# A three-stage attention and expert kernel: the second expert's first nine weights held back until the last float64 tile is converted

## The chip, the cores and the metric

The kernel runs on one core of a Trainium2 chip. A core has five engines that run side by side and wait for each other by semaphores: TensorE (PE in the profile; PEld is its weight load), VectorE (DVE), ScalarE (ACT), GpSimd (POOL) and SyncE (SP, which here only issues transfers). The metric is the time of one execution on the device, in microseconds; less is better.

## The reference

Linear attention with decay, then a mixture of experts with capacity, then a dense two-layer network. Cut to what matters:

```python
# attention over t: y_t = r_t (state + u k_t v_t);  state = w state + k_t v_t
x = attn_out.transpose(0, 2, 1, 3).reshape(3072, 384)
# greedy routing: each of 8 experts takes 384 tokens, the highest gate values first
for e in range(8):
    mask = assigned == e
    out[mask] = relu(x[mask] @ w1[e]) @ w2[e]        # 384 -> 1024 -> 384
h = relu(out @ w_in)                                  # 384 -> 2048
return ((h * h) @ w_out)                              # 2048 -> 384
```

The weights w1 and w2 are float32 and each belongs to one expert. The weights w_in and w_out are float64, and all tokens share them.

## The kernel before

The kernel first computes the attention in 24 chunks of 128 tokens. It then takes the eight experts one after the other, in an order that the routing finds out on the way. For each it routes (`phase`), gathers that expert's 384 tokens, runs the expert's two layers (`expert`) and at once the dense network on the same tokens (`mlp`), and scatters the 384 rows to the output.

Every operand of a product is split in two parts: a rounded one (`wh`, `ah`, `YH`, `WI[0]`) and the rest (`wl`, `al`, `YL`, `WI[1]`), the difference to the full value. `mm3` multiplies rounded by rounded, rounded by rest and rest by rounded: lines 836, 837 and 838. A block of one 128-wide column of weights against 384 tokens is nine such matmuls.

**Expert weights.** Each expert has 16 tiles of 128x384 numbers, eight of w1 (`n` 0 to 7) and eight of w2 (`n` 8 to 15). In the list `seq` the first expert has the numbers 0 to 15 and the second 16 to 31. `load_next` issues the next tile's transfer from SP into one of five raw buffers (line 921), as soon as routing knows which expert comes (`known`). `split_next` makes the two parts in one of nine pairs of buffers: the rounded part on ACT (line 832) and the rest on POOL (line 833; the first eight on DVE). It puts both 200 places ahead in the priorities of the planner that orders the queues of ACT, DVE and POOL. SP and PE keep the order in which the program is written. In expert 1 (the second) the block `hmm(1, f)` needs the tile 16+f, and `ymm(1, 0)`, which stands right behind `hmm(1, 2)`, needs tile 24, the ninth.

**float64 weights.** The dense network's weights are 32 tiles of float64 (`wi` 0 to 15 and `wo` 0 to 15, taken in turn). They are turned into float32 once, while the first expert and its dense network run, and are then kept. `fetch` loads a tile from SP (line 856). `convert` has three pieces on DVE (lines 886, 887, and 883 in `join`, which completes the number), then the rounded part on ACT (872) and the rest on POOL (868). `fill` hands out the pieces, three per step in the first expert and two per step in its dense network. A step is a call of `tick`, which also calls `load_next` and `split_next`. Counted through the program, the second expert becomes known in step 32, and the last piece of the last float64 tile is handed out in step 35. Step 38 is followed by the block `gmm` 13 of the first dense network, step 40 by `gmm` 14 and step 42 by `gmm` 15, and expert 1 begins after step 47.

In the dense network the block `gmm(p, f)` needs both parts of `wi` f and `omm(p, f)` those of `wo` f, in the order `omm(0)`, `gmm(4)`, `omm(1)`, `gmm(5)`, ... `omm(11)`, `gmm(15)`, `omm(12)` to `omm(15)`. Between `gmm` and `omm` stand three steps on ACT (1006, 1012, 1013) and one on DVE (1016, `al`). `oev` then scatters three times 128 rows from POOL (1031). The routing of the following expert runs beside all this, mostly in small steps on DVE.

Of the kernel before, what the change touches and what calls it, by code (L numbers as in the profile page):

```python
# [42 lines left out]
FB1, FB2 = 8, 16  # L43
KG = 64
BIG = 1e38
NW, NRAW = 9, 5
# [749 lines left out]
def moe(ctx, tc, a, R, xd, out):  # L796
    nc = tc.nc
    V, G, A_, PE = nc.vector, nc.gpsimd, nc.scalar, nc.tensor
# [14 lines left out]
    now, queue = [-1], []  # L813

    def later(k, fn):
        if now[0] < 0:
            fn()
        else:
            queue.append((now[0] + k, fn))
# [11 lines left out]
    def split(t, hi, lo, eng=None):  # L831
        A_.activation(hi, t, AF.Copy)  # L832
        (eng or G).tensor_tensor(lo, t, hi.bitcast(FT), op=OP.subtract)  # L833
# [7 lines left out]
    WI = [cs.tile([128, FB2, 3, 128], FR, name=f"wi{j}") for j in range(2)]  # L841
    WO = [cs.tile([128, FB2, DM], FR, name=f"wo{j}") for j in range(2)]
    order = [x for f in range(FB2) for x in (("wi", f), ("wo", f))]
    fetched, pieces, rest, done, alive, hold, credit = [], [], {}, set(), [], [False], [0.0]

    def part(w, f, j):
        return WI[j][:, f].rearrange("p k m -> p (k m)") if w == "wi" else WO[j][:, f]
# [12 lines left out]
    def convert(w, f, t):  # L860

        hi, lo = part(w, f, 0), part(w, f, 1)
        wide = t.dtype == I32
        v = t[:, :, 1].bitcast(FT) if wide else t

        def end():
            def finish():
                G.tensor_tensor(lo, v, hi.bitcast(FT), op=OP.subtract)  # L868
                done.add((w, f))
                alive.pop()  # L870

            todo = rest[w, f] = [lambda: A_.activation(hi, v, AF.Copy), finish]  # L872
            go = lambda: todo and todo.pop(0)()
            later(1, go)
            later(2, go)

        if not wide:
            return [end]
        low, high = t[:, :, 0], t[:, :, 1]
        c = ps.tile([128, 512], I32, name="conv", bufs=1)[:, :384]  # L880

        def join():
            V.scalar_tensor_tensor(high, high, -1073741824, c, op0=OP.bitwise_and, op1=OP.bitwise_or)
            end()

        return [lambda: V.tensor_scalar(c, high, 5, 2, op0=OP.logical_shift_left, op1=OP.logical_shift_right),
                lambda: V.scalar_tensor_tensor(c, low, 29, c, op0=OP.logical_shift_right, op1=OP.bitwise_or),
                join]

    def fill(n=1):  # L890
        credit[0] += n
        while credit[0] >= 1:
            credit[0] -= 1
            if not pieces:
                fetch()
                if not fetched:
                    return
                pieces.extend(convert(*fetched.pop(0)))
                fetch()
            pieces.pop(0)()  # L900
# [11 lines left out]
    raws, wt, used, loaded_at = {}, {}, set(), {}  # L912

    def load_next():
        i = len(loaded_at)
        if i >= len(seq) or i >= len(wt) + NRAW or not st[seq[i][0]].get("known"):
            return False
        p, n = seq[i]
        src = a["w1"] if n < FB1 else a["w2"]
        raws[i] = rawp.tile([128, 384], FT, name="raw")  # L920
        nc.sync.dma_start(raws[i], src[bass.ds(st[p]["e"], 1), n % FB1].rearrange("a p m -> (a p) m"))
        loaded_at[i] = now[0]
        return True

    def split_next(eng=None, wait=2):
        i = len(wt)
        if i >= len(loaded_at) or (i >= NW and i - NW not in used) or now[0] < loaded_at[i] + wait:
            return False
        wt[i] = wp.tile([128, 384], FR, name="wh"), wp.tile([128, 384], FR, name="wl")
        with tc.high_priority(offset=200 if now[0] >= 0 else 0):  # L930
            split(raws[i], *wt[i], eng=eng or (V if i < 8 else G))
        return True

    def weight(p, n):
        i = at[p, n]
        while i >= len(wt):
            load_next()
            split_next(wait=-9)
        return wt[i]
# [4 lines left out]
    def tick():  # L944
        now[0] += 1
        run_due(now[0])
        with tc.high_priority(offset=100 if rate[0] else 0):
            if now[0] >= 11:
                next(bg[0], None)
        if rate[0]:  # L950
            fill(rate[0])
        while load_next():
            pass
        split_next(wait=4)
# [140 lines left out]
    with tc.manual_schedule():  # L1095
        first = True
        for ev in route(0):
            if ev == "expert":
                hold[0] = True
                while load_next():  # L1100
                    pass
            if ev == "gather":
                fill(6)
                warm(16)
                for _ in range(NRAW):
                    split_next(wait=-9)
            if ev == "x":
                warm(3)
                if first:
                    while load_next():  # L1110
                        pass
                first = False
        hold[0] = False
        fetch()
        for _ in range(4):
            split_next(wait=-9)
            load_next()
# [14 lines left out]
@with_exitstack  # L1132
def tile_attention_moe_mlp(ctx: ExitStack, tc: tile.TileContext, a, out):
    nc = tc.nc
    cp = ctx.enter_context(tc.tile_pool(name="persist", bufs=1))
    dp = ctx.enter_context(tc.tile_pool(name="scratch", bufs=1, space=bass.MemoryType.DRAM))
    xd = dp.tile([NT * 128, DM], FT, name="xd")
    rp = ctx.enter_context(tc.tile_pool(name="route", bufs=2))
    L = cp.tile([128, NT, E], FT, name="L")
    R = Routing(tc, rp, cp.tile([128, 128], FT, name="ident"), L)  # L1140
    with ExitStack() as inner:
        inner.enter_context(tc.manual_schedule())
        attention(inner, tc, a, R, L, xd)
    moe(ctx, tc, a, R, xd, out)
# [56 lines left out]
```

## Time and profile before

| what | value |
|---|---|
| median of 3 runs | 813.88 us (813.44 to 814.23) |
| profiled execution, its own time | 816.39 us |
| profiled execution, span from first to last instruction | 814.4 us |
| mean granted clock of TensorE over the span | 0.966 |
| PE busy | 782.1 us (96%) |
| DVE, ACT, POOL busy | 410.5, 380.1, 304.8 us |

The span lies 2.0 us below the profiled execution's own time, and the median of the three runs 2.5 us below that time. Times in rows are counted from the start of the span. A granted clock of 1.00 is 2.4 GHz and 0.50 is 1.2 GHz.

### The profile page before, as it was taken

How to read it: one execution, taken by the hardware profiler on the slowest of the kernel's cores; microseconds unless marked ns; L12 is line 12 of the kernel's file. 1: busy time of each engine (PE TensorE's matmuls, PEld its weight loads, DVE VectorE, ACT ScalarE, POOL GpSimd, SP SyncE). 2: the span in 40 equal slices, each digit the busy share in tenths (PEclk: the TensorE clock that was granted, in tenths of full speed). 3: DMA queues.
4: the chain of work that ended last, by engine and by line, in shares of the span. 5: the costliest groups of instructions: out<-in, count | busy, mean ns of one | idle time of the engine just before them, and what ended most of it. 6: DMA issues, size and time to landing. Idle time of an engine off the chain costs nothing.

```text
span 814.4 us, 15971 instructions
## 1 busy us (share of the span) xinstructions
PE 782.1 (96%) x6078; PEld 733.2 (90%) x6078; DVE 410.5 (50%) x1077; ACT 380.1 (47%) x883; POOL 304.8 (37%) x323
## 2 busy tenths in 40 slices
PE   8999998699978999999999999999999999999996
PEld 5888885498968999999999999999999999999996
DVE  6588875988883464157314731573255213211210
ACT  3556551256654256426542654264426445433442
POOL 7788841275574214312330234032404153104001
PEclk8799996699998999999999999999999999999999
DMA  8697711475452014102310321032104132101000
GB/s 246 201 324 238 235 61 39 123 246 158 144 183 70 20 51 116 49 2 70 97 49 1 88 79 49 1 99 68 50 1 126 41 101 84 30 1 50 1 1 29
DMA packets 37499, 73.69 MB, mean 90 GB/s; under 512 B 5568, under 2 KB 25264, under 8 KB 37424
## 3 DMA queue, kind: packets, MB, share of 16 engines
q1 hardware_dynamic: 34352, 63.25, 26.0%
q0 software_dynamic: 3072, 9.44, 3.5%
q8 instruction: 47, 0.77, 0.4%
q14 instruction: 28, 0.23, 0.1%
HBM read 63.24 MB, written 9.44 MB: 89 GB/s over the span
## 4 chain that ended last, share of the span: by engine, by line
PE 86%; issue 4%; DVE 3%; POOL 3%; DMA 2%; ACT 1%; SPq 0%; POOLq 0%; DVEq 0%; ACTq 0%
PE acc L836 12%; PE ph L836 11%; PE acc L838 11%; PE acc L837 11%; PE ph L838 11%; PE ph L837 11%; PE pA L213 4%; PE pY L232 3%; DMA raw<-in_w_dram 2%; PE pt L269 2%; PE pl L249 2%; PE pY L225 2%; PE ph L968 1%; POOL wi L868 1%; PE pk L292 1%
## 5 line engine op out<-in xcount | busy, mean ns | idle before, releaser
L833 POOL TENSOR_TENSOR wl<-raw,wh 128x384 fp32r<-128x384 f32 x120 | 121.1, 1025 | 188.5 <-ACT wh L832 185.6
L836 PE MATMUL ph<-YH,wi 128*128 128x384 f32 x384 | 133.5, 348 | 4.2 <-ACT wi L872 4.2
L1016 DVE TENSOR_TENSOR al<-ph,ah 128x384 fp32r<-128x384 f32 x113 | 62.9, 557 | 146.3 <-ACT ph L1013 144.9
L838 PE MATMUL ph<-YH,wi 128*128 128x384 f32 x384 | 130.2, 339 | 3.8 <-POOL wi L868 3.8
L836 PE MATMUL acc<-wo,ah 128*128 128x384 f32 x384 | 131.3, 342 | 0.0
L838 PE MATMUL acc<-wo,al 128*128 128x384 f32 x384 | 129.3, 337 | 1.0 <-POOL al L1016 1.0
L1006 ACT ACTIVATE t<-ph 128x384 f32<-128x384 f32 x128 | 61.7, 488 | 145.6 <-PE ph L838 138.4
L837 PE MATMUL ph<-YL,wi 128*128 128x384 f32 x384 | 129.3, 337 | 0.0
L837 PE MATMUL acc<-wo,ah 128*128 128x384 f32 x384 | 129.0, 336 | 0.0
L1031 POOL DMA_INDIRECT out_dram<-rows,idx x24 | 23.7, 987 | 220.2 <-ACT rows L1029 216.0
L832 ACT ACTIVATE wh<-raw 128x384 fp32r<-128x384 f32 x128 | 65.6, 522 | 71.2 <-DMA raw<-in_w_dram 22.0
L976 DVE SCALAR_TENSOR_TENSOR al<-ph,ah 128x384 fp32r<-128x384 f32 x64 | 35.6, 556 | 87.8 <-ACT ah L975 87.7
L836 PEld LDWEIGHTS ph<-YH,wi 128*128 128x128 f32 x384 | 72.8, 190 | 4.8 <-ACT wi L872 4.8
L838 PEld LDWEIGHTS ph<-YH,wi 128*128 128x128 f32 x384 | 72.8, 190 | 4.5 <-POOL wi L868 4.5
L838 PEld LDWEIGHTS acc<-wo,al 128*128 128x128 f32 x384 | 72.5, 189 | 1.7 <-POOL al L1016 1.4
L836 PEld LDWEIGHTS acc<-wo,ah 128*128 128x128 f32 x384 | 72.8, 190 | 0.0
L837 PEld LDWEIGHTS ph<-YL,wi 128*128 128x128 f32 x384 | 72.8, 190 | 0.0
L837 PEld LDWEIGHTS acc<-wo,ah 128*128 128x128 f32 x384 | 72.7, 189 | 0.0
L1012 ACT ACTIVATE ah<-t 128x384 fp32r<-128x384 f32 x128 | 67.1, 524 | 2.5
L836 PE MATMUL acc<-ah,wh 128*128 128x384 f32 x192 | 66.1, 344 | 0.0
L837 PE MATMUL acc<-al,wh 128*128 128x384 f32 x192 | 64.5, 336 | 1.0 <-DVE al L976 1.0
L838 PE MATMUL acc<-ah,wl 128*128 128x384 f32 x192 | 64.4, 336 | 0.0
(239 smaller groups left out, 1519.9 us busy)
## 6 DMA issues: line engine op xcount, KB each, us to landing
raw<-in_w_dram SPq DMA_DIRECT2D x128, 192.0 KB, 2.6
rk<-in_rk_dram SPq DMA_DIRECT2D x24, 448.0 KB, 5.5
tk<-in_tk_dram SPq DMA_DIRECT2D x24, 392.0 KB, 5.8
raw<-in_wi_dram SPq DMA_DIRECT2D x16, 384.0 KB, 3.7
raw<-in_wo_dram SPq DMA_DIRECT2D x16, 384.0 KB, 3.7
xd<-xs SPq DMA_DIRECT2D x24, 192.0 KB, 2.6
rows<-xd,idx POOLq DMA_INDIRECT x24
out_dram<-rows,idx POOLq DMA_INDIRECT x24
```

The lines of the kernel that those rows point to most:

```text
L213: PE.matmul(pA[n][s][:, i], RK[n][half(s), 1, i], RK[n][half(s), 0, i], start=True, stop=True)
L232: PE.matmul(pYs[n][s][half(i % 2, 64), i // 2], v_of(n, 2 * i + s), AM[n][:, i, s], start=not c and i < 2, stop=True, skip_group_check=True)
L832: A_.activation(hi, t, AF.Copy)
L833: (eng or G).tensor_tensor(lo, t, hi.bitcast(FT), op=OP.subtract)
L836: PE.matmul(o, l[0], r[0], start=first, stop=False)
L837: PE.matmul(o, l[0], r[1], start=False, stop=False)
L838: PE.matmul(o, l[1], r[0], start=False, stop=last)
L976: later(1, lambda: V.scalar_tensor_tensor(hl, o, 0.0, hh.bitcast(FT), op0=OP.max, op1=OP.subtract))
L1006: A_.activation(t, o, AF.Relu)
L1012: A_.activation(gh, t, AF.Square)
L1016: later(2, lambda: (G if p == 0 and f < 8 else V).tensor_tensor(gl, t2, gh.bitcast(FT), op=OP.subtract))
L1031: h = G.indirect_dma_start(out=out, out_offset=bass.IndirectOffsetOnAxis(ap=st[p]["idx"][:, i:i + 1], axis=0), in_=t, in_offset=None)
```

## The change

`load_next` no longer issues tiles 16 to 24 when the expert is known: it waits in program order until no float64 tile is left to fetch, to begin or to piece together. For tile 16 it also adds a copy of one number on DVE, from the float64 tile converted last into the raw buffer that the transfer will fill, so that on the chip the transfer waits for that DVE instruction, and with it all the later transfers of SP. `split_next` gives tiles 16 to 24 no precedence any more, and makes the rest of the odd ones (17, 19, 21, 23) on DVE; the even ones stay on POOL. By the same count the first transfers move from step 32 to step 35, and the nine splits from steps 36 to 44 to steps 39 to 47.

```diff
+    final = []
...
         c = ps.tile([128, 512], I32, name="conv", bufs=1)[:, :384]
+
+        final[:] = [v]
...
     def load_next():
...
+        if 2 * FB1 <= i < 2 * FB1 + NW and (order or fetched or pieces):
+            return False
         p, n = seq[i]
         src = a["w1"] if n < FB1 else a["w2"]
         raws[i] = rawp.tile([128, 384], FT, name="raw")
+        if i == 2 * FB1 and final:
+            V.tensor_copy(raws[i][0:1, 0:1], final[0][0:1, 0:1])
         nc.sync.dma_start(raws[i], src[bass.ds(st[p]["e"], 1), n % FB1].rearrange("a p m -> (a p) m"))
...
     def split_next(eng=None, wait=2):
...
+        second = 2 * FB1 <= i < 2 * FB1 + NW
         wt[i] = wp.tile([128, 384], FR, name="wh"), wp.tile([128, 384], FR, name="wl")
-        with tc.high_priority(offset=200 if now[0] >= 0 else 0):
-            split(raws[i], *wt[i], eng=eng or (V if i < 8 else G))
+        with tc.high_priority(offset=200 if now[0] >= 0 and not second else 0):
+            split(raws[i], *wt[i], eng=eng or (V if i < 8 or second and i % 2 else G))
```

## Rows read from the trace of the kernel before

**Rows 1.** Waits of PE from 160 us to the end: total, times, longest.
```profile
PE ph L836 <- ACT wi L872: 4.2, 2, 3.4
PE ph L838 <- POOL wi L868: 3.8, 2, 2.8
```

**Rows 2.** Windows: length, each engine's busy time (instructions), clock, DMA share, GB/s.
```profile
226.20:227.40 1.20, 0.22 (x3) 0.01 (x1) 1.20 (x4) 0.41 (x2) 0.71 (x1) 1.00 0.70 269
...
234.15:239.40 5.25, 0.80 (x4) 0.31 (x3) 2.61 (x8) 3.17 (x8) 3.38 (x5) 1.00 0.69 230
239.40:242.70 3.30, 3.30 (x10) 3.30 (x11) 3.30 (x8) 1.54 (x4) 3.30 (x4) 0.51 0.46 130
...
248.20:253.10 4.90, 4.89 (x16) 4.79 (x17) 0.85 (x2) 1.78 (x4) 0.94 (x1) 0.50 0.16 50
```

**Rows 3.** Timeline of PE: start, duration, instruction, idle time before it and releaser.
```profile
233.98 0.34 PE L838 MATMUL acc<-wo,al 128*128 128x384 f32 x1
237.77 0.45 PE L836 MATMUL ph<-YH,wi 128*128 128x384 f32 x1 [3.45 <-ACT wi L872]
...
239.39 0.65 PE L838 MATMUL ph<-YH,wi 128*128 128x384 f32 x1 [1.00 <-POOL wi L868]
...
244.75 0.44 PE L836 MATMUL ph<-YH,wi 128*128 128x384 f32 x1 [0.75 <-ACT wi L872]
...
248.21 0.69 PE L838 MATMUL ph<-YH,wi 128*128 128x384 f32 x1 [2.84 <-POOL wi L868]
...
259.04 0.33 PE L968 MATMUL ph<-XH,wh 128*128 128x384 f32 x1
...
263.72 0.33 PE L836 MATMUL acc<-ah,wh 128*128 128x384 f32 x1
```

**Rows 4.** Timeline of ACT in the same stretch.
```profile
233.32 0.53 ACT L1012 ACTIVATE ah<-t 128x384 fp32r<-128x384 f32 x1
235.07 0.52 ACT L832 ACTIVATE wh<-raw 128x384 fp32r<-128x384 f32 x1 [1.23 <-DMA raw<-in_w_dram]
...
237.18 0.53 ACT L872 ACTIVATE wi<-raw 128x384 fp32r<-128x384 f32 x1
```

**Rows 5.** Timeline of POOL in the same stretch.
```profile
233.44 1.04 POOL L868 TENSOR_TENSOR wo<-raw,wo 128x384 fp32r<-128x384 f32 x1
...
243.30 3.89 POOL L833 TENSOR_TENSOR wl<-raw,wh 128x384 fp32r<-128x384 f32 x4
247.15 1.01 POOL L868 TENSOR_TENSOR wi<-raw,wi 128x384 fp32r<-128x384 f32 x1
```

**Rows 6.** Timeline of DVE in the same stretch.
```profile
232.52 0.55 DVE L883 SCALAR_TENSOR_TENSOR raw<-raw,conv 128x384 int32<-128x384 int32 x1
...
233.71 0.82 DVE L621 TENSOR_TENSOR key<-m,dead 128x24 f32<-128x24 f32 x1
...
239.36 0.56 DVE L1016 TENSOR_TENSOR al<-ph,ah 128x384 fp32r<-128x384 f32 x1 [2.64 <-ACT ph L1013]
...
241.40 0.54 DVE L883 SCALAR_TENSOR_TENSOR raw<-raw,conv 128x384 int32<-128x384 int32 x1
...
243.24 0.56 DVE L883 SCALAR_TENSOR_TENSOR raw<-raw,conv 128x384 int32<-128x384 int32 x1
```

**Rows 7.** Timeline of SP's queue from 231.5 us: the expert tiles' transfers.
```profile
231.20 2.18 SPq L921 DMA_DIRECT2D raw<-in_w_dram  x4
```

**Rows 8.** Transfers issued in 230:238 and in 238:262: KB each, us to landing.
```profile
raw<-in_w_dram SPq DMA_DIRECT2D x6, 192.0 KB, 4.9
...
raw<-in_w_dram SPq DMA_DIRECT2D x8, 192.0 KB, 2.6
```

**Rows 9.** Groups by line: busy us, mean ns of one, idle time before.
```profile
L833 POOL TENSOR_TENSOR wl<-raw,wh 128x384 fp32r<-128x384 f32 x120 | 121.1, 1025 | 188.5 <-ACT wh L832 185.6 <-PE acc L838 2.2
...
L833 DVE TENSOR_TENSOR wl<-raw,wh 128x384 fp32r<-128x384 f32 x8 | 4.0, 548 | 0.8 <-ACT wh L832 0.8
...
L755 DVE CAST dat<-o 128x1 f16<-128x1 f32 x7 | 1.0, 146 | 0.0
```

## The prediction

> **What bounds the kernel now.** I read the page first. PE is 96% busy and no other engine more than half, so only time in which PE waits, or runs at the lower clock, can be won. The waits of PE from the first expert on show where [rows 1]: of what stops it, 8.0 us are two blocks of the first dense network that wait for a float64 weight, half for ACT's rounded part, half for POOL's rest. All the later blocks run without a break, so the rest of the kernel should simply move with the end of this stretch. Then I took the windows around those waits [rows 2] and the timeline of each engine in them [rows 3 to 7].
>
> PE finishes `omm(10)` at 234.15 (233.98 and one pitch) and begins expert 1 at 259.04 [rows 3]. The pitch of a 384-column matmul at full clock is 0.173 us: from 259.04 to 263.72 stand three blocks, 27 matmuls in 4.68 us. Between 234.15 and 259.04 stand `gmm(14)`, `omm(11)`, `gmm(15)` and `omm(12)` to `omm(15)`, 63 matmuls, and nine smaller transposes: at most 72 pitches, 12.5 us. The stretch takes 24.9, so at least 12.4 us are lost. Two thirds are the gaps of 3.45, 1.00, 0.75 and 2.84 us [rows 3]. The rest is clock: behind each pair of gaps PE runs at 0.51 and 0.50, that is at 1.2 GHz, ten matmuls in 3.30 us and sixteen in 4.90 [rows 2].
>
> Who is late? DVE completes `wi` 14 at 233.07 [rows 6]. ACT is free at 233.85, but next in its queue stand two expert tiles whose transfers have not landed: it starts them at 235.07 and 236.75 and comes to `wi` 14 at 237.18 [rows 4]. On DVE an `al` then waits 2.64 us for ACT, and the next float64 piece is behind it, so that `wi` 15 is complete only at 241.94 [rows 6]. Then four rests of expert tiles, 3.89 us, keep POOL from `wi` 15 until 247.15 [rows 5]. The tiles that get in the way are not needed before 259.04.
>
> **The change, part by part.**
>
> *Holding the transfers and taking away the precedence.* Tile 16 cannot be on ACT before the last float64 tile is complete on DVE, so the tiles leave the queues ahead of `wi` 14 and 15. I work the stretch out again with the same durations. `wi` 14: complete 233.07, ACT free 233.85 at the latest, done at about 234.3; POOL finishes `wo` 13 at 234.5 [rows 5] and then takes 1.0 for the rest, 235.5. PE loses 0.2 before the block and 0.7 at its third matmul. It runs the other seven (1.2) and `omm(11)` (1.6) and stands before `gmm(15)` at 238.3. `wi` 15: without DVE's 2.64 us of waiting its completion moves from 241.94 to 239.3; ACT 239.9, POOL 240.9. PE loses 1.6 before that block and 0.6 in it. In all 3.1 of the 12.4 remain: **9.3 us gained**. Expert 1 begins at about 249.7.
>
> The clock: the remaining loss of 1.6 and 0.6 lies between a row of 1.2 us with little work, after which the clock is 1.00, and one of 5.25 us, after which it is 0.51 [rows 2]. It is nearer the first; I take no slow stretch, and keep 1.6 us (ten matmuls in 3.30 instead of 1.73) as the upper bound.
>
> *What is late next: the nine tiles.* Step 35 hands out the last piece; DVE completed it at 243.80 [rows 6], and 2.6 earlier, at 241.2, in the new order. The copy of one number is like the smallest copy shown, 0.15 us [rows 9]; its lower bound is nothing and its upper one 1.0, below. It is on no path of PE. SP then issues at 0.55 us each (four in 2.18, [rows 7]): 241.4 to 243.6. Nothing else of SP is queued behind: all float64 fetches precede. Landing took 2.6 us in calm and 4.9 among float64 tiles and gathered rows [rows 8]; these are through by then, so I take 2.6: first tile 244.0. Each then needs 0.5 on ACT [rows 4], and 1.03 on POOL or 0.55 on DVE [rows 9]. Tile 16 is done at 245.7, which lets tile 21's transfer go; likewise 22, 23 and 24, the last at 247.4 and landing at 250.0. Tile 24 is split by 251.7, 10.4 us after the copy. Tile 16 is needed at 249.7, 4 us after it is ready. The ninth is needed at the third matmul of `ymm(1, 0)`, 4.68 and two pitches later, 254.7. So nothing is lost, with 3 us to spare; with slow landings (2.3 more, twice) it would be 2 us late.
>
> *The rests on DVE.* The four odd ones take 2.2 us of DVE, which idles by then, instead of 4.1 of POOL. They are hidden by the 3 us to spare, and would cost nothing without it, as POOL would take longer. One row speaks against: DVE's `key<-m,dead`, 24 numbers with both operands in SBUF, took 0.82 us beside POOL's `wo` 13 and ended with it, at 234.5 [rows 5, 6]. If the odd rests and the copy are held like that until POOL's current instruction ends, the nine rests run one after the other, 7.4 us instead of 5.2, and the ninth comes 1 to 2 us later, still within the 3. The Trainium skill states such a rule (GPSIMD Engine Reference, Key points): GpSimd shares its SBUF interfaces with VectorE and contends with VectorE instructions that have two SBUF inputs. By that rule, which the row bears out, splitting the rests over the two engines gives less than their durations promise; the time would be the same here, the case of late tiles likelier.
>
> *The sum.* 9.3 us of the profiled execution's 816.39 is 807.1. That execution is 2.5 us above the median of the three runs, so on the median it is 813.88 - 9.3 = **804.6 us**.
>
> **The rivals.**
>
> *Tiles too late.* If the planner puts the copy on DVE behind work that waits for PE, such as the last `al` or the rests of expert 1's rows (243 to 249 in the new times), the tiles shift with it. From a copy at 244.3 each microsecond is one of waiting at `ymm(1, 0)`, and 1.6 to 2.1 of slow clock come on top. Three slow landings, or the three scatters on POOL (which begin when `mlp` ends, near 249.7) ahead of the last even rests, come to the same. For it: the copy and splits have no precedence any more, and the first raw buffers carry all nine. Against it: 3 us to spare. Price 2 to 7, time 807 to 811.
>
> *VectorE is the real bound.* DVE has no idle time in the 6.75 us up to `omm(10)`, as its rows lie end to end, and the next routing steps stand between the float64 pieces. If these delay `wi` 15 further, by some 2 us, and the slow clock follows (1.6), the gain is 5.7: 808.2. Against it: DVE waited 2.64 us there for ACT, and that wait goes.
>
> *More than the sum.* With ACT and POOL free, the planner may also bring the float64 pieces forward, and nearly all 12.4 us go, up to the point where the tiles set the pace: 11 to 12, time 802.
>
> *Slower.* The same wait of `ymm(1, 0)`, grown past the gain. In the kernel before that block begins at 263.72; with 10.4 us from copy to ninth rest, and 2.1 of slow clock behind the wait, a copy later than about 251.6 loses time. This is so if it is queued behind the routing counts of the following expert, which need all of expert 1's transposes first. At 254 the time is 816. For it: one DVE instruction in a queue that a planner orders holds all nine transfers. Against it: its operand is ready at 241 and it is written ahead of all that work.
>
> *Nothing changes.* ACT and POOL could be late for other reasons than the tiles. Rows 4 and 5 show the tiles themselves in the gap, so I give it little.
>
> **How the numbers follow.** The forecast's own case, a gain of 7.5 to 11, time 803 to 806.4: 0.48. More than the sum, 801.2 to 803: 0.10. Tiles too late, 807 to 811: 0.12. VectorE, around 808: 0.10. Those are the faster cases, 0.80. Within 0.2% (1.6 us, about what a measurement of this kernel can tell from no change): 0.07. Slower: 0.13, the copy far back or the planner's order elsewhere worse. The range from 801.2 to 811 holds the four faster cases; the other 0.20 lies above.
>
> **What would show it.** In the profile after: no line-832 instruction on ACT and no line-833 one on POOL between `wi` 14 and `wo` 15; the idle time of PE before the two blocks down from 8.0 to about 3, and the granted clock at 1.00 after it; a one-element copy on DVE near 241, line 921 on SP right behind it; four line-833 instructions on DVE; PE at line 968 near 249.7 and the first `acc<-ah,wh` 4.7 later without a wait. The span should shrink by what that start moves. I am wrong if that `ymm` block waits for `wl`, if an engine's queue shows a tile waited for ahead of something PE needs, or if the later experts show waits that they did not have.

## The result, and the profile after

The changed kernel takes 805.46 us (median of five runs, 805.15 to 808.93), against 814.23 of the kernel before in the same series: a ratio of 0.990, 95% interval 0.988 to 0.993. That is 8.8 us less; 804.6 was forecast, and 805.46 lies in its range. The profiled execution took 805.15 us, with a span of 803.4 and a mean granted clock of 0.979.

In the rows below, lines after the diff have moved: the copy is line 927, the transfer 928, the float64 pieces 889, 890 and 886, their rounded part 873 and rest 869, `al` of the dense network 1024, the scatters 1039, `hmm` 976. First the waits of PE from 160 us on, the groups with more than 0.9 us in all:

```profile
PE ph L836 <- ACT wi L873: 2.9, 2, 1.9
PE acc L838 <- POOL al L1024: 1.0, 1, 1.0
PE ph L838 <- POOL wi L869: 1.0, 2, 0.5
```

Beside [rows 1], the 8.0 us before `gmm(14)` and `gmm(15)` are 3.9. The timeline of PE says where:

```profile
230.95 0.34 PE L838 MATMUL acc<-wo,al 128*128 128x384 f32 x1
...
232.28 0.44 PE L836 MATMUL ph<-YH,wi 128*128 128x384 f32 x1 [0.99 <-ACT wi L873]
...
233.38 0.44 PE L838 MATMUL ph<-YH,wi 128*128 128x384 f32 x1 [0.49 <-POOL wi L869]
...
238.31 0.44 PE L836 MATMUL ph<-YH,wi 128*128 128x384 f32 x1 [1.89 <-ACT wi L873]
...
239.41 0.44 PE L838 MATMUL ph<-YH,wi 128*128 128x384 f32 x1 [0.48 <-POOL wi L869]
...
248.00 0.33 PE L976 MATMUL ph<-XH,wh 128*128 128x384 f32 x1
...
252.68 0.33 PE L836 MATMUL acc<-ah,wh 128*128 128x384 f32 x1
...
253.03 0.38 PE L838 MATMUL acc<-ah,wl 128*128 128x384 f32 x1
```

From the end of `omm(10)`, 231.12, to expert 1 at 248.00 are 16.88 us, where [rows 3] have 24.89: **8.0 us of gain in the stretch that the forecast was about**. From there to expert 1's first dense block both kernels take the same, 27.02 before and 27.06 after, and the 4.68 to `ymm(1, 0)` are unchanged. The two profiled executions differ by 11.2 us, though. The other 3.0 lie before the stretch (`omm(10)` ends that much earlier), where PE runs the same instructions in the same order: a difference between executions, no part of the change. The granted clock from 100 to 145 us was 0.84 in the profile before and 0.89 in this one; the version late_splits_again below has 0.83 there and ends `omm(10)` at 233.95, nearly as late as the kernel before (234.15). The medians' 8.8 is nearer the stretch.

The windows (length, each engine's busy time and instructions, granted clock, DMA share, GB/s) show that PE ran at 2.4 GHz throughout; [rows 2] have 0.51 and 0.50 behind the waits:

```profile
234.15:239.40 5.25, 2.89 (x16) 2.26 (x14) 4.12 (x12) 2.27 (x5) 2.04 (x2) 1.00 0.00 0
239.40:242.70 3.30, 3.29 (x20) 3.23 (x21) 1.16 (x6) 2.32 (x6) 1.03 (x1) 1.00 0.47 139
...
248.20:253.10 4.90, 4.90 (x30) 4.81 (x29) 3.87 (x6) 3.66 (x10) 4.45 (x5) 1.00 0.73 241
```

On ACT no expert tile stands before the last float64 tile any more, other than in [rows 4]:

```profile
231.67 0.55 ACT L873 ACTIVATE wi<-raw 128x384 fp32r<-128x384 f32 x1 [0.48 <-DVE raw L886]
...
237.72 0.54 ACT L873 ACTIVATE wi<-raw 128x384 fp32r<-128x384 f32 x1 [1.09 <-DVE raw L886]
239.71 0.55 ACT L873 ACTIVATE wo<-raw 128x384 fp32r<-128x384 f32 x1 [1.45 <-DVE raw L886]
242.52 0.52 ACT L832 ACTIVATE wh<-raw 128x384 fp32r<-128x384 f32 x1
```

In the three rows of line 873 ACT waits for DVE. The timeline of DVE has what it waits for (beside [rows 6]), the copy, and the four rests that moved:

```profile
229.73 1.44 DVE L618 TENSOR_TENSOR lm<-L,pen 128x192 f32<-128x192 f32 x1
231.10 0.54 DVE L886 SCALAR_TENSOR_TENSOR raw<-raw,conv 128x384 int32<-128x384 int32 x1
...
236.66 0.56 DVE L1024 TENSOR_TENSOR al<-ph,ah 128x384 fp32r<-128x384 f32 x1 [1.09 <-ACT ph L1021]
237.14 0.55 DVE L886 SCALAR_TENSOR_TENSOR raw<-raw,conv 128x384 int32<-128x384 int32 x1
...
239.71 0.14 DVE L927 COPY raw<-raw 1x1 f32<-1x1 f32 x1
...
244.17 0.55 DVE L833 TENSOR_TENSOR wl<-raw,wh 128x384 fp32r<-128x384 f32 x1
245.56 1.01 DVE L833 TENSOR_TENSOR wl<-raw,wh 128x384 fp32r<-128x384 f32 x1 [0.84 <-ACT wh L832]
248.06 0.55 DVE L833 TENSOR_TENSOR wl<-raw,wh 128x384 fp32r<-128x384 f32 x1
249.72 1.25 DVE L833 TENSOR_TENSOR wl<-raw,wh 128x384 fp32r<-128x384 f32 x1
```

On POOL, against [rows 5], nothing stands before `wi` 15, but the scatters of the first expert's rows have come between the last rests:

```profile
229.91 1.04 POOL L869 TENSOR_TENSOR wo<-raw,wo 128x384 fp32r<-128x384 f32 x1
...
238.34 1.01 POOL L869 TENSOR_TENSOR wi<-raw,wi 128x384 fp32r<-128x384 f32 x1 [1.41 <-ACT wi L873]
...
248.26 1.24 POOL L1039 DMA_INDIRECT out_dram<-rows,idx  x1 [0.16 <-issue]
249.53 1.02 POOL L833 TENSOR_TENSOR wl<-raw,wh 128x384 fp32r<-128x384 f32 x1
250.72 1.13 POOL L1039 DMA_INDIRECT out_dram<-rows,idx  x1 [0.17 <-issue]
251.87 1.03 POOL L833 TENSOR_TENSOR wl<-raw,wh 128x384 fp32r<-128x384 f32 x1
```

The last of these rows is the ninth tile, ready at 252.90; `ymm(1, 0)` uses it at 253.03. SP's queue answers to [rows 7]:

```profile
239.88 16.56 SPq L928 DMA_DIRECT2D raw<-in_w_dram  x16
```

and the transfers issued in 231 to 245 us to [rows 8] (count, KB each, median us to landing):

```profile
raw<-in_w_dram SPq DMA_DIRECT2D x7, 192.0 KB, 2.9
```

### The profile page after: what moved, and what is told of

It is laid out like the page before. It is cut to its first block, busy times and chain, and to the rows that moved or that the text cites. A ratio compares the mean times of both kernels' runs of the same rounds, so it can differ in the third digit from the quotient of the medians.

```text
span 803.4 us, 15976 instructions
## 1 busy us (share of the span) xinstructions
PE 772.2 (96%) x6078; PEld 724.9 (90%) x6078; DVE 411.6 (51%) x1082; ACT 380.2 (47%) x883; POOL 300.9 (37%) x319
## 4 chain that ended last, share of the span: by engine, by line
PE 84%; issue 4%; POOL 4%; DMA 3%; DVE 3%; ACT 0%; SPq 0%; POOLq 0%; DVEq 0%; ACTq 0%
PE acc L836 12%; PE ph L836 11%; PE acc L838 11%; PE acc L837 11%; PE ph L838 11%; PE ph L837 11%; PE pA L213 3%; PE pY L232 3%; DMA rk<-in_rk_dram 2%; PE pl L249 2%; PE pt L269 2%; PE pY L225 2%; PE ph L976 1%; POOL wi L869 1%; POOL wo L869 1%
## 5 line engine op out<-in xcount | busy, mean ns | idle before, releaser
L833 POOL TENSOR_TENSOR wl<-raw,wh 128x384 fp32r<-128x384 f32 x116 | 116.6, 1021 | 187.8 <-ACT wh L832 123.4
```

## The experiments

Two numbers of each profile serve throughout: the **stretch** from the end of `omm(10)` to expert 1, and the **way**, the stretch and expert 1's own time up to its first dense block, which also holds whatever is given back there. Waits are those of PE before `gmm(14)` for ACT and for POOL, then the same two before `gmm(15)`. All edits are against the changed kernel. "Ratio" is to the kernel before in the same series, whose median was 813.19 from prec_only to late_splits, 814.04 from changed_again to reload_3, and 815.78 in the last four rows.

| kernel | median, us | ratio [95%] | stretch | way | waits |
|---|---|---|---|---|---|
| before | 814.23 | | 24.89 | 51.91 | 3.45, 1.00, 0.75, 2.84 |
| changed | 805.46 | 0.990 [0.988, 0.993] | 16.88 | 43.94 | 0.99, 0.49, 1.89, 0.48 |
| prec_only | 811.45 | 0.997 [0.996, 0.999] | 21.61 | 48.62 | 0.42, 0.49, 2.70, 2.80 |
| hold_in_program | 812.79 | 1.000 [0.999, 1.002] | 23.35 | 50.36 | 2.50, 0.74, 1.05, 1.76 |
| rests_on_pool | 808.60 | 0.994 [0.992, 0.996] | 18.06 | 45.42 | 0.98, 0.49, 1.89, 0.32 |
| late_splits | 804.16 | 0.988 [0.986, 0.990] | 15.29 | 42.31 | 0.53, 0.48, 0.72, 0.50 |
| changed_again | 807.27 | 0.992 [0.990, 0.994] | 18.48 | 45.50 | 0.98, 0.49, 1.89, 0.48 |
| later_routing | 805.82 | 0.991 [0.989, 0.993] | 15.23 | 43.87 | 0.42, 0.84, 0.42, 0.48 |
| late_splits_later_routing | 805.43 | 0.990 [0.988, 0.992] | 16.27 | 43.29 | 0, 0.80, 0.42, 0.49 |
| reload_3 | 816.64 | 1.003 [1.001, 1.005] | 19.67 | 54.36 | 1.00, 0.48, 1.88, 0.48 |
| late_splits_again | 804.94 | 0.988 [0.985, 0.990] | 15.24 | 42.26 | 0.51, 0.48, 0.72, 0.49 |
| later_routing_ninth | 804.87 | 0.988 [0.986, 0.990] | 15.29 | 42.59 | 0.42, 0.88, 0.42, 0.49 |
| later_routing_rests | 806.06 | 0.989 [0.987, 0.991] | 13.94 | 42.46 | 0.42, 0, 0.52, 0 |
| changed_third | 806.24 | 0.990 [0.988, 0.991] | 18.50 | 45.51 | 1.00, 0.49, 1.89, 0.48 |

**One part of the change at a time.** The theory was that tiles ahead in the queues of ACT and POOL cost the time, and that the wait on the chip is what removes them. Against it stood that the precedence alone does it, or the order of the program, or that early transfers disturb the float64 ones.

The precedence alone (`prec_only`): no hold, all rests on POOL.

```diff
-        if 2 * FB1 <= i < 2 * FB1 + NW and (order or fetched or pieces):
-            return False
...
-        if i == 2 * FB1 and final:
-            V.tensor_copy(raws[i][0:1, 0:1], final[0][0:1, 0:1])
...
-            split(raws[i], *wt[i], eng=eng or (V if i < 8 or second and i % 2 else G))
+            split(raws[i], *wt[i], eng=eng or (V if i < 8 else G))
```

> Only the precedence is taken away: the nine tiles are loaded as early as before, SP waits for nothing, all rests on POOL. Queue theory (the 8 us of the stretch from omm(10) to expert 1 come from tiles standing ahead of wi 14 and wi 15 on ACT and POOL): the planner's queues now have wi 14 ahead of the tiles, but still five roundings on ACT and five rests on POOL between wi 14 and wo 14, and two more of each ahead of wi 15. So the loss before gmm 14 shrinks as in the changed kernel and that before gmm 15 stays: the stretch takes 19 to 23 us instead of 24.9 (before) and 16.9 (changed), gain 2 to 6 us. Precedence theory (taking away the precedence is what helps, the hold is not needed): the same time as the changed kernel, gain 8 to 9. Transfer theory (the tiles' early transfers collide with the float64 tiles' and the gathered rows'): no gain, as the transfers stay where they were.

It gives about a fifth of the gain, 1.7 us in the medians. `wi` 14 now comes before the tiles on ACT, but two tiles still stand before `wi` 15, the second of them waiting for its transfer (timeline of ACT):

```profile
231.45 0.53 ACT L873 ACTIVATE wi<-raw 128x384 fp32r<-128x384 f32 x1
231.89 0.51 ACT L832 ACTIVATE wh<-raw 128x384 fp32r<-128x384 f32 x1
...
236.76 0.51 ACT L832 ACTIVATE wh<-raw 128x384 fp32r<-128x384 f32 x1
237.87 0.52 ACT L832 ACTIVATE wh<-raw 128x384 fp32r<-128x384 f32 x1 [0.60 <-DMA raw<-in_w_dram]
238.30 0.54 ACT L873 ACTIVATE wi<-raw 128x384 fp32r<-128x384 f32 x1
```

POOL made two rests there too, 1.97 us from 239.31, before `wi` 15's.

The hold in the order of the program alone (`hold_in_program`): the copy is left out, the condition stays.

```diff
-        if i == 2 * FB1 and final:
-            V.tensor_copy(raws[i][0:1, 0:1], final[0][0:1, 0:1])
```

> The changed kernel without the copy of one number: the transfers stand behind the last float64 piece in the order of the program only, and nothing holds SP on the chip. SP's order is the same as before, so on the chip the tiles are loaded as early as before. Queue theory: the planner then places one tile ahead of wi 14 on ACT and POOL and four each ahead of wo 14 and wi 15, so most of the loss is back: stretch 20 to 25 us, gain 0 to 5, clearly slower than the changed kernel. If the place in the program were what counts: as the changed kernel, gain 8 to 9.

Nothing that can be measured is left of the gain: the profiled way is 1.6 us shorter, but the interval of the ratio leaves 1.2 at most. Without the copy the transfers start at 228.05, before `omm(10)` ends, and ACT has a tile, waiting for its transfer, before `wi` 14 again, and four before `wi` 15 (timeline of ACT):

```profile
232.51 0.52 ACT L832 ACTIVATE wh<-raw 128x384 fp32r<-128x384 f32 x1 [1.58 <-DMA raw<-in_w_dram]
232.94 0.53 ACT L873 ACTIVATE wi<-raw 128x384 fp32r<-128x384 f32 x1
...
239.44 1.75 ACT L832 ACTIVATE wh<-raw 128x384 fp32r<-128x384 f32 x4
241.09 0.54 ACT L873 ACTIVATE wi<-raw 128x384 fp32r<-128x384 f32 x1
```

So the change does not work without the copy of one number, 0.14 us of DVE. The copy alone, with the precedence kept, was not run.

All nine rests on POOL (`rests_on_pool`):

```diff
-            split(raws[i], *wt[i], eng=eng or (V if i < 8 or second and i % 2 else G))
+            split(raws[i], *wt[i], eng=eng or (V if i < 8 else G))
```

> The changed kernel with all nine rests on POOL; everything else as changed. Queue theory with the tiles in time: the ninth rest is ready at the latest 2 to 3 us later than with four on DVE, and PE may wait up to 2 us at the first ymm block of expert 1; stretch from omm(10) to expert 1 as changed, 16.9. Gain 6 to 9. If the odd rests on DVE are an essential part (POOL is the bound in that stretch): a wait of more than 3 us at that ymm block, gain under 5.

The waits are those of the changed kernel, but for 0.24 us at `ymm(1, 0)`, whose third matmul starts at 253.97 where its place was 253.73. Its stretch is longer by 1.2 us because PE ran slower behind the waits, with a granted clock of 0.63 from 238.90 to 242.50. As the next runs show, the changed kernel does so too in most of its profiles, so that of the difference in the medians only the 0.24 can be put down to the rests with some right.

The transfers early, the roundings held (`late_splits`): the hold and the copy of `load_next` go, and instead the `wh` buffer of each of the nine tiles first gets one number from the last float64 tile, so that the tile's rounding on ACT can't come before that.

```diff
-        if 2 * FB1 <= i < 2 * FB1 + NW and (order or fetched or pieces):
-            return False
...
-        if i == 2 * FB1 and final:
-            V.tensor_copy(raws[i][0:1, 0:1], final[0][0:1, 0:1])
...
         wt[i] = wp.tile([128, 384], FR, name="wh"), wp.tile([128, 384], FR, name="wl")
+        if second: V.tensor_copy(wt[i][0][0:1, 0:1], final[0][0:1, 0:1])
```

> The nine tiles are loaded as early as before, next to the last float64 tiles and the gathered rows, but each rounding on ACT waits for a one-number copy on DVE from the float64 tile completed last into its target. Queue theory: as the changed kernel or slightly better, gain 7 to 10, since ACT and POOL are free of the tiles and they are ready earlier. Transfer theory: the collision of transfers is back, so the gain shrinks to 0 to 3.

> The kernel with early loads and held roundings once more, beside the changed kernel on the same chip: if it is really better, 1 to 3 us below the changed kernel; its stretch from omm(10) to expert 1 near 15.3 us with the clock at 1.00 throughout. If its lead came from the chip or from luck with the clock: equal within 1 us.

In late_splits the transfers start 3.5 us before `omm(10)` ends (232.14), as in the kernel before (timeline of SP):

```profile
228.65 27.49 SPq L928 DMA_DIRECT2D raw<-in_w_dram  x16
```

With them as early as that, this is no worse than the changed kernel. The rival that the early transfers collide with the float64 ones falls: what counts is when the tiles stand in ACT's and POOL's queues. It is even better by 1.6 us of stretch, since the planner now puts `wi` 15's last piece ahead of the `al` that waits for PE's block (timeline of DVE, where `al` is one line further on; in the changed kernel they stand the other way round):

```profile
236.32 0.54 DVE L886 SCALAR_TENSOR_TENSOR raw<-raw,conv 128x384 int32<-128x384 int32 x1
237.24 0.56 DVE L1025 TENSOR_TENSOR al<-ph,ah 128x384 fp32r<-128x384 f32 x1 [0.38 <-ACT ph L1022]
```

**The changed kernel again**, beside the other kernels of each series.

> The changed kernel once more, as the measure for the other runs of this call: gain 8 to 9 us, stretch from omm(10) to expert 1 near 16.9 us. The waits before gmm 15 (1.89 and 0.48 us in its first profile) may or may not be followed by a stretch at 1.2 GHz, worth about 1.2 us, as in the run with all rests on POOL, where the same waits were followed by one.

> The changed kernel as the measure for this call: gain 7 to 9 us over the kernel before. Waits before gmm 14 and gmm 15 of 0.98, 0.49, 1.89 and 0.48 us again; with a stretch at 1.2 GHz behind them 18.0 to 18.5 us from omm(10) to expert 1, without one 16.9.

The gain holds: 0.992 and 0.990. Both profiles show the same four waits as the first, to 0.01 us, but a stretch longer by 1.6. The windows of changed_third have the reason:

```profile
239.50:242.00 2.50, 1.94 (x7) 1.62 (x8) 1.65 (x8) 0.58 (x2) 1.41 (x2) 0.77 0.00 0
242.00:244.00 2.00, 2.00 (x9) 1.90 (x9) 0.00 (x0) 0.66 (x2) 0.63 (x1) 0.50 0.81 227
244.00:246.00 2.00, 2.00 (x14) 1.97 (x13) 1.12 (x2) 1.56 (x4) 0.36 (x1) 0.93 0.78 238
246.00:250.00 4.00, 4.00 (x25) 3.96 (x24) 3.19 (x6) 3.16 (x7) 2.70 (x3) 1.00 0.46 133
```

PE is busy all the time from 242.00 to 244.00 and gets 9 matmuls done, at 1.2 GHz. In five profiles with these waits (changed, rests_on_pool, changed_again, reload_3, changed_third) the clock fell in four. Both late_splits profiles, with 0.72 us in place of the 1.89, kept 1.00 after the waits.

**The slower rival, brought about.** Tile 16 is loaded four times, so that the other tiles come later (`reload_3`).

```diff
-        nc.sync.dma_start(raws[i], src[bass.ds(st[p]["e"], 1), n % FB1].rearrange("a p m -> (a p) m"))
+        for _ in range(4 if i == 2 * FB1 else 1): nc.sync.dma_start(raws[i], src[bass.ds(st[p]["e"], 1), n % FB1].rearrange("a p m -> (a p) m"))
```

> The changed kernel with tile 16 loaded four times into the same buffer, one after the other, before the second tile goes: three more landings of 2.6 to 3.0 us, all nine tiles some 8 to 9 us later, nothing else changed but the planner's order for the later tiles. The ninth tile was ready 0.1 us before its use. If every microsecond of lateness beyond that is one of waiting: PE waits 6 to 9 us in the first three blocks of expert 1 and runs up to 2 us more at 1.2 GHz behind them, so that the time is within 2 us of the kernel before, and slower than the changed kernel by 7 to 10. If the tiles have slack that the profile does not show: less than 4 us lost.

Three transfers more, and the whole gain is gone: 9.4 us above the changed kernel of that series. Timeline of PE:

```profile
252.02 0.44 PE L976 MATMUL ph<-XH,wh 128*128 128x384 f32 x1 [0.99 <-ACT wh L832]
...
255.45 0.69 PE L976 MATMUL ph<-XH,wl 128*128 128x384 f32 x1 [2.99 <-POOL wl L833]
...
264.61 0.45 PE L838 MATMUL acc<-ah,wl 128*128 128x384 f32 x1 [0.92 <-POOL wl L833]
```

The way is 8.9 us longer than in changed_again. 4.9 of it are these three waits, less than the 6 to 9 expected, and behind the second PE ran at 1.2 GHz, with a granted clock of 0.50 from 255.45 to 261.06. Part of it is the order on POOL: with the tiles late, all three scatters stand before the first rest (timeline of POOL).

```profile
250.79 1.01 POOL L1039 DMA_INDIRECT out_dram<-rows,idx  x1 [8.18 <-ACT rows L1037]
...
254.40 2.91 POOL L833 TENSOR_TENSOR wl<-raw,wh 128x384 fp32r<-128x384 f32 x3
```

**What the remaining waits hang on.** ACT waited for DVE, so the third expert's routing, whose small steps stand between the float64 pieces, was put behind them: its first step also waits for the last float64 tile (`later_routing`).

```diff
                 lm = w(sh, "lm", FT, 1)
+                if p == 2: V.tensor_copy(lm[0:1, 0, 0:1], self.final[0][0:1, 0:1])
...
-    final = []
+    R.final = final = []
```

> The changed kernel, and the first steps of the routing for the third expert (lines 618 to 621 and 467 to 470, some 3.5 us of VectorE between the last float64 pieces) wait for a one-number copy from the last float64 tile. If VectorE is what bounds the remaining 3.9 us of waits before gmm 14 and gmm 15: the wait before gmm 15 falls from 2.4 to under 1 us, the stretch from 16.9 to 14.5 to 15.5, 1.5 to 2.5 us better than the changed kernel. If ACT or POOL still bound it, or the routing is then late: no better than the changed kernel.

> Both together: tiles loaded early, their roundings held back until the last float64 tile is completed, and the third expert's routing behind that tile as well. If the tiles cost only by their place on ACT and POOL and VectorE bounds the rest: stretch 14 to 15 us, as good as or better than either alone, gain over before 10 to 11 us. If early transfers cost anything next to the last float64 tiles: worse than the later routing alone.

The waits for ACT go from 2.88 to 0.84 and the stretch to 15.23, so what held them is the order on VectorE. The median, 805.82, is 1.4 us below changed_again's, with intervals that overlap. The way is 43.87, no shorter than in the first profile of the changed kernel: `ymm(1, 0)` now waits for the ninth rest, which POOL has behind the three scatters (timeline of PE; lines are one further on).

```profile
253.08 0.44 PE L839 MATMUL acc<-ah,wl 128*128 128x384 f32 x1 [1.01 <-POOL wl L834]
```

Expert 1 takes 28.64 us to its dense block, 1.6 more than in the changed kernel, at a granted clock of 1.00. So the "0.6 of clock" in the expectation of later_routing_ninth is not clock. The second matmul of `ymm(1, 0)` starts 0.2 late, for `al`, and the rest lies around the wait, which its row counts 0.3 short (the account of the waits that remain, below, says how).

With late_splits as well, `omm` waits 1.24 us for an `al` on DVE instead; the two do not add up.

So, beside that, the ninth rest goes to DVE (`later_routing_ninth`, the first edit below), and then also those of `wi` 14 and 15 (`later_routing_rests`, both):

```diff
-            split(raws[i], *wt[i], eng=eng or (V if i < 8 or second and i % 2 else G))
+            split(raws[i], *wt[i], eng=eng or (V if i < 8 or second and (i % 2 or i == 24) else G))
```

```diff
-                G.tensor_tensor(lo, v, hi.bitcast(FT), op=OP.subtract)
+                (V if w == 'wi' and f > 13 else G).tensor_tensor(lo, v, hi.bitcast(FT), op=OP.subtract)
```

> The kernel with the third expert's routing behind the last float64 tile, and the ninth tile's rest on VectorE too. If the 1.0 us of waiting and 0.6 of clock at the first ymm block came from that rest standing behind scatters on POOL: both go, expert 1 takes 27.0 us to its gmm again, total 1 to 2 us better than the kernel with later routing and 2 to 3 better than the changed one. If the tile itself is late: the wait stays.

> The same with the rests of wi 14 and wi 15 on VectorE as well (0.55 instead of 1.03 us each). The waits before gmm 14 and gmm 15, 0.42 + 0.84 and 0.42 + 0.48, lose about 0.9 in all: stretch 14.2 to 14.6 instead of 15.2, the best of the study, gain 10 to 11 over before. If VectorE is then the bound: no better than with POOL.

The first takes the wait at `ymm(1, 0)` away (way 42.59). The second brings the stretch to 13.94, the shortest of all, with both waits for POOL gone, and gives 1.5 us back at `ymm(1, 0)`, where PE now waits 1.23 us for DVE's `al`; its median is no better. **The versions that do best** are late_splits (804.16 and 804.94) and later_routing_ninth (804.87), all at a ratio of 0.988 against the changed kernel's 0.990 to 0.992. In the one series that holds both beside the changed kernel they are 1.3 and 1.4 us below it; the intervals overlap in part, so this is a likely gain and no more.

## Why the prediction was right

**The cause: right; its size: too large.** Two thirds of the loss were gaps behind the tiles in ACT's and POOL's queues. With the tiles held on the chip the stretch is 8.0 us shorter in the first pair of profiles, and 6.4 in the two where the clock fell; 9.3 was forecast. prec_only and hold_in_program show that neither the precedence nor the program's order does it, late_splits that it is not the transfers.

**The waits that remain: 4.7 instead of 3.1.** The rows give 3.85, but they count a wait from the end of the row before, 0.33 or 0.34 us after its start. The forecast counted from one pitch after that start, which is 0.16 earlier; so counted, the four are 1.16, 0.75, 2.05 and 0.75. `wi` 14 was to be complete 1.1 us before the end of `omm(10)` and was so 0.5 after it, 1.1 of these 1.6 because `lm<-L,pen` took 1.44 us on DVE until POOL's `wo` rest had ended. In later_routing the same instruction, away from POOL's rests, took 0.36:

```profile
238.92 0.36 DVE L619 TENSOR_TENSOR lm<-L,pen 128x192 f32<-128x192 f32 x1
```

`wi` 15 came at 6.6 us after that end instead of 5.1, its last piece behind the `al`. In late_splits, where that order is turned round, the wait is 0.72 instead of 1.89. So the rival that VectorE is the real bound was largely true: its order holds what remains, as later_routing shows, and `wi` 15 was 1.5 us later than the sum had it, where the rival said 2. Where the clock fell as well, the stretch's gain of 6.4 is nearer the rival's 5.7 than the sum's 9.3.

**Work: 12.2 instead of 12.5.** 16.88 less 4.7 is 12.2. The nine transposes took less than nine pitches. The second matmul after each of the four gaps starts 0.27 or 0.28 us behind the first, not one pitch of 0.17; the sum had counted pitches alone.

**The clock: the step that failed, though the first profile bore it out.** The forecast took no slow stretch, with 1.6 us as the bound, because the remaining waits looked nearer to a row of 1.00. In the first profile the clock stayed at 1.00; in changed_again and changed_third, with the same waits, it fell, and the stretch was 1.60 and 1.62 us longer. With rests_on_pool and reload_3 that is four profiles of five: the bound was right and the choice was not. That this is also what spreads the changed kernel's runs over 805.2 to 809.7 is argued, as runs without a profile show no windows.

**The ninth tile: 0.1 us to spare instead of 3.** The copy came 8.6 us after the end of `omm(10)` (7.0 forecast), and the landing took 2.9 and 2.7 (2.6). But from copy to ninth rest were 13.2 us instead of 10.4. The forecast had the even rests on POOL end to end, and put the scatters ahead of them only in the rival with late tiles. The planner set two between the last three rests (1.24 and 1.13 us). ACT had rounded the ninth tile by 250.04, but its rest began at 251.87, behind the second scatter; that is 1.8 of the 2.8. Two of DVE's four rests took 1.01 and 1.25 instead of 0.55; that they delayed the ninth is not shown. Nothing was lost, but any further delay is paid, as reload_3 shows: this is the slower rival, and it needs no more than three transfers.

**The rests on DVE: a small part.** Moving them was to be worth nothing; it is worth 0.24 us at `ymm(1, 0)`. With the ninth on DVE too, the wait of later_routing there (1.01) is gone.

**The sum.** 9.3 was put against a median of 813.88, and the medians gave 8.8. The stretch alone gives 8.0 in the first pair of profiles and 6.4 in the two with a slow clock (24.89 less 18.5). The medians of the three series differ by 8.8, 6.8 and 9.5. That 805.46 came so near the 804.6 is in part luck: the waits were under-counted by 1.6 us, and the slow clock, left out, came in two of the changed kernel's three profiles.

## What to carry to other kernels

A planner fixes the order of the in-order queues before anything has landed (that it goes by estimated landing times is argued; no run shows its estimates). Where a transfer lands late, the instruction that waits for it holds back everything behind it, also work whose data is there. A tiny copy that makes the early work depend on the late one on the chip mended this, where moving it in the program's order did not. Put the dependence on the work that stands in the queue and not on its transfer, and look at once at what is just in time behind it: here 0.1 us was left.

## What the runs showed of the hardware

- VectorE's instructions with two operands in SBUF were held by GpSimd's: `lm<-L,pen` 1.44 us against 0.36, the rests 1.01 and 1.25 against 0.55, and the held ones end 0.2 to 0.4 us behind an element-wise instruction of POOL (its rest 249.53 to 250.55, the DVE row 249.72 to 250.97). The Trainium skill names such a contention (GPSIMD Engine Reference, Key points); the rows agree with it and add the price, up to 1.1 us each.
- The holding goes both ways. Where a rest of POOL began during one of DVE's, it was POOL's that took longer: in late_splits two of three took 1.34 and 1.33 us instead of 1.02, so that the three (timeline of POOL) took 3.60, where three in the kernel before took 3.06. The rest of DVE at 248.06 ran its 0.55 us beside a scatter that had begun after it; that scatter took 1.24 us, and the one beside the end of the rest at 249.72 took 1.13, against 0.99 for the third, beside none, and 0.97 to 1.01 in the kernel before. That DVE held the scatters is argued from these two.

```profile
241.67 3.60 POOL L833 TENSOR_TENSOR wl<-raw,wh 128x384 fp32r<-128x384 f32 x3 [0.46 <-ACT wh L832]
```

- The same waits, 0.98 to 1.00, 0.48 or 0.49, 1.88 or 1.89 and 0.32 to 0.48 us in five profiles, were followed once by a clock of 1.00 and four times by a fall to 1.2 GHz that cost 1.2 to 1.6 us. In this case the clock behind a wait could not be told from the waits.
